# An attention and mixture block on one core: TensorE order written by hand, V mixed a batch ahead, residual in place, and a new order of loads

## The chip, the cores and the metric

One core of one Trainium2 chip runs the kernel. The metric is the time of one execution on the device in microseconds (us). Before the change it is 268.94 us (median of four runs, 268.52 to 269.49).

A time is given with the granted clock of TensorE, the mean over the span of what the trace records (in the traces of before and after, each record is 1 or 0.5). A run is called slow when it lies more than 1.5% above the fastest run of the same kernel. On one core that label is only about times. A median is over all runs, a ratio over the fast ones.

## The reference, cut to what matters

```
# batch 4, heads 8, seq 768, head_dim 64, 8 blocks of 96 rows
P = sort_net                                  # [4, 8, 8, 8]
5 times: P = exp(P - max); P /= rowsum; P /= colsum
k_sorted, v_sorted = P applied to the 8 blocks of k and of v
attn = softmax(q_block @ k_sorted_block.T / 8)
x = (attn @ v_sorted_block), heads side by side             # [4, 768, 512]
a1 = alpha1 * x + beta1
u  = x + lam * (w_tok @ a1)                   # token mixing, w_tok [768, 768]
a2 = alpha2 * u + beta2
out = u + lam * (relu(a2 @ w_ch1) @ w_ch2)    # channel stage, hidden 2048
```

The inputs and the output are float32. The kernel works in 16-bit types on TensorE.

## The kernel before

Names used in this text: `raw` is k or v as loaded; `bigP`, `bigV` are the mixing matrices made of P; `kT`, `Vs` are mixed k (transposed) and mixed v; `sc_ps` scores; `et` their exponentials; `x` the attention result; `tok_ps` token mixing; `u` the residual; `a2T` its transposed affine copy; `h_ps`, `hT` the hidden layer; `W2p` is w_ch2; `ch_ps` the channel result. P.V is the product of `et` and `Vs`. A filler (`spin`) is a matmul whose result nobody uses; `gate` is a tiny GpSimd copy that only holds back the loads queued behind it until what it reads has arrived. In the profiles PE is TensorE (PEld its weight loads), DVE VectorE, ACT ScalarE, POOL GpSimd.

Every compute engine is wrapped: while `fixed` is true its instructions keep program order, and with `fixed = False` the compiler may reorder them. GpSimd (`pool`) issues most loads. SyncE (`nc.sync`) issues the stores, the round trip of V through a scratch in memory (`vscr`), and the DMA transposes.

```python
    def load_weights():                       # called early in batch 0
        for g in range(4):
            pool.dma_start(W1p[...g...], w1v[...g...])
        load_raw(1, 1)                        # v of batch 1
        for g in range(4):
            pool.dma_start(W2p[...g...], w2v[...g...])

    def mix_v(b, banks=2, groups=range(6), copies=...):
        ...  # matmuls raw x bigV -> v_ps, copied to vA
        for th in range(2):
            nc.sync.dma_start(vscr[b, ...th...], vA[...th...])
        for par in range(2):
            regroup[b] = nc.sync.dma_start(Vs[b % NV][...par...], vscr[b]...)

    def emit_attention(b):                    # batches 1 to 3
        ...
        prev = [emit_scores(b, 0, g) for g in range(2)]
        for h4 in range(1, H4):
            cur = [emit_scores(b, h4, g) for g in range(2)]
            emit_pv(b, h4 - 1, prev, x128, xs)
            ...

    def moe_ch(b, hf, kks=range(3)):
        ...
            ost = att.tile([128, C], FT, name="ost", tag="ost", bufs=2)
            ...  # 16 matmuls hT x W2p into cps
                dve.tensor_tensor(cps[:], cps[:], lamB[:, lo:hi], ALU.mult)
                dve.tensor_tensor(ost[:, lo:hi], cps[:], u_of[b][kt][:, lo:hi], ALU.add)
                ...  # ost stored by SyncE

    pe.fixed = False                          # the compiler's order from here
    for b in range(1, B):
        if b > 1:
            if b > 2:
                cross_q(b)                    # six DMA transposes of q on SyncE
            mixing_matrices(b)
            mix_v(b)
            if b == 2:
                ...                           # gate, then load_q(3), load_raw(3, 1), load_raw(3, 0)
            mix_k(b)
        emit_attention(b)
        if b == 1:
            moe_ch(0, 0, (2,))
        else:
            moe_h(b - 1, 0)
            moe_ch(b - 1, 0)
        moe_h(b - 1, 1)
        moe_a(b)                              # token mixing, u, transposes of u
        moe_ch(b - 1, 1)
        if b == 1:
            load_q(2)
            cross_q(2)
    for hf in range(2):
        moe_h(B - 1, hf)
        moe_ch(B - 1, hf)
```

The softmax here doesn't subtract the row's maximum and nothing guards it: scores larger than these inputs give would overflow.

## Time and profile before

| | before |
|---|---|
| time, median (range) | 268.94 us (268.52 to 269.49) |
| span of the profiled run | 266.8 us |
| mean granted clock | 1.000 |
| first token-mixing matmul of batch 0, 1, 2, 3 | 33.96, 85.25, 144.03, 202.81 us |
| last matmul ends | 262.66 us |

The last two rows come from the timeline of TensorE. I use the first token-mixing matmul of each batch as milestones and call the times between them stretches: 51.3 us from batch 0 to 1 (of which the first 8.7 belong to batch 0's token mixing, up to the first h at 42.64 us), 58.8, 58.8, and 59.9 us from the last milestone to the end.

First, the busy rows of the page. The first line is the engine's busy time, share and instruction count; the digits are the busy share in 40 equal slices of the span (one slice is 6.7 us); PEclk is the granted clock in tenths and DMA the busy share of the DMA engines.

```profile
PE 257.6 (97%) x2049; PEld 141.6 (53%) x2059; DVE 154.8 (58%) x333; ACT 125.8 (47%) x232; POOL 92.5 (35%) x100
...
PE   7799999999999999999999999999999999999993
...
PEclk9999999999999999999999999999999999999999
DMA  6999999999999544499996342494200432012012
```

TensorE is the bottleneck and it is never long without work after the first slice; its clock stays at full. The DMA engines are over 90% busy in slices 2 to 13, from 7 to 87 us.

The waits of TensorE (engine, tile, the instruction that released it; then total us, times, longest us) are short. The whole kernel has no matmul wait over 1.4 us:

```profile
PE spin_ps L65 <- POOL ident L65: 1.4, 1, 1.4
PE pj_ps L65 <- DVE P L65: 1.2, 1, 1.2
```

Two groups of the page's fifth part (busy us and mean ns, then idle us just before the group and who ended it). The channel matmuls wait for nothing. GpSimd's rows of `u` wait for VectorE's `ost`:

```profile
L65 PE MATMUL ch_ps<-W2p,hTa 128*128 128x512 bf16 (+2 forms) x290 | 65.9, 370 | 0.5
...
L65 POOL TENSOR_SCALAR u<-b1lB,rs 128x512 f32<-128x512 f32 x18 | 28.8, 1610 | 64.1 <-DVE ost L65 59.3
```

Busy time by stage (windows; the stage's edges, its length, then each engine's busy time and instruction count, the clock, and the DMA engines' time as a share):

```profile
core 0: us, PE busy (x) PEld busy (x) DVE busy (x) ACT busy (x) POOL busy (x), PEclk, DMA share, GB/s
34.00:43.00 9.00, 9.00 (x57) 4.38 (x54) 7.33 (x15) 5.79 (x10) 8.17 (x8) 1.00 1.16 210
43.00:85.00 42.00, 41.80 (x389) 24.73 (x391) 28.68 (x58) 24.87 (x48) 18.29 (x20) 1.00 1.29 182
85.00:144.00 59.00, 58.69 (x420) 30.88 (x421) 35.47 (x72) 28.47 (x53) 25.75 (x26) 1.00 0.92 131
144.00:203.00 59.00, 58.69 (x420) 30.85 (x420) 35.11 (x71) 28.31 (x53) 16.64 (x13) 1.00 0.42 70
```

The loads that matter later are those of W2, four of 512 KB, as GpSimd issues them. This is its timeline (start, duration, engine, operation):

```profile
27.31 1.54 POOL L65 DMA_DIRECT2D W2p<-in_moe_w_ch_dram  x2
29.09 0.75 POOL L65 DMA_DIRECT2D W2p<-in_moe_w_ch_dram  x1 [0.24 <-DMA W1p<-in_moe_w_ch_dram]
31.60 0.74 POOL L65 DMA_DIRECT2D W2p<-in_moe_w_ch_dram  x1 [1.76 <-DMA W1p<-in_moe_w_ch_dram]
```

They landed between 42.62 and 50.24 us. The first channel matmul needs them at 55.2 us.

### The profile page before, as it was taken

To read this page: it belongs to the slowest core of one execution; us is meant where nothing else is said; L and a number is where in the kernel's file an instruction comes from. 1 tells how busy PE (TensorE), PEld (TensorE's weight loads), DVE (VectorE), ACT (ScalarE), POOL (GpSimd) and SP (SyncE) were. 2 spreads that over 40 slices of the span, in tenths; PEclk is the share of its full clock that TensorE was granted. 3 is DMA by queue.
4 is the path that set the end of the run, shared out by engine and by line. 5 is a ranking of instruction groups with operands and counts; after the bars stand their busy time and mean duration, and the time that the engine had idled before them with its cause. 6 is when DMAs were issued, how large, how long until landed. Compare 5 with 4: busy or idle time off the path is not lost.

```text
span 266.8 us, 5149 instructions
## 1 busy us (share of the span) xinstructions
PE 257.6 (97%) x2049; PEld 141.6 (53%) x2059; DVE 154.8 (58%) x333; ACT 125.8 (47%) x232; POOL 92.5 (35%) x100
## 2 busy tenths in 40 slices
PE   7799999999999999999999999999999999999993
PEld 2467745565565444554565444554565445545542
DVE  5878788629567966722585966704675962042033
ACT  3376757643585312980375404970474305504600
POOL 8524689203575615007917225002409000000000
PEclk9999999999999999999999999999999999999999
DMA  6999999999999544499996342494200432012012
GB/s 83 174 208 251 207 210 207 211 216 112 211 157 155 113 84 117 114 82 89 202 211 136 61 100 80 118 98 62 80 2 2 81 76 79 2 39 79 2 39 79
DMA packets 62423, 30.88 MB, mean 116 GB/s; under 512 B 48888, under 2 KB 58112, under 8 KB 62400
## 3 DMA queue, kind: packets, MB, share of 16 engines
q0 software_dynamic: 23024, 15.60, 39.4%
q1 hardware_dynamic: 39280, 14.89, 32.6%
q8 instruction: 16, 0.26, 0.4%
q14 instruction: 7, 0.06, 0.1%
q10 hardware_dynamic: 96, 0.07, 0.1%
HBM read 32.78 MB, written 8.65 MB: 155 GB/s over the span
## 4 chain that ended last, share of the span: by engine, by line
PE 89%; ACT 4%; DVE 4%; issue 1%; DMA 1%; DVEq 0%; ACTq 0%
PE ch_ps L65 31%; PE h_ps L65 30%; PE tok_ps L65 12%; PE x_ps L65 5%; PE sc_ps L65 4%; ACT kT L65 2%; PE v_ps L65 2%; PE k_ps L65 1%; PE q_ps L65 1%; ACT et L65 1%; DVE csum L65 1%; DVE P L65 1%; PE m_ps L65 1%; DVE rsum L65 1%; DMA P<-in_sort_net_dram 1%
## 5 line engine op out<-in xcount | busy, mean ns | idle before, releaser
L65 PE MATMUL h_ps<-a2T,W1p 128*128 128x384 bf16 x512 | 93.4, 326 | 0.1
L65 ACT ACTIVATE hTa<-h_ps 128x384 bf16<-128x384 f32 x96 | 45.9, 492 | 68.1 <-PE h_ps L65 67.0
L65 PE MATMUL ch_ps<-W2p,hTa 128*128 128x512 bf16 (+2 forms) x290 | 65.9, 370 | 0.5
L65 PEld LDWEIGHTS <-W1p 128*128 128x128 bf16 x512 | 47.5, 98 | 30.3 <-issue 0.9
L65 DVE TENSOR_TENSOR ch_ps<-ch_ps,lamB 128x512 f32<-128x512 f32 (+2 forms) x25 | 16.9, 676 | 63.2 <-PE ch_ps L65 60.5
L65 POOL TENSOR_SCALAR u<-b1lB,rs 128x512 f32<-128x512 f32 x18 | 28.8, 1610 | 64.1 <-DVE ost L65 59.3
L65 PEld LDWEIGHTS <-hTa 128*128 128x128 bf16 x300 | 28.7, 98 | 32.4
L65 PE MATMUL tok_ps<-x,w_tokT 128*128 128x512 f16 x144 | 32.1, 379 | 0.0
L65 POOL TENSOR_TENSOR u<-x,u 128x512 f32<-128x512 f16 x22 | 25.3, 1181 | 18.1 <-DVE x L65 17.3
L65 ACT ACTIVATE et<-sc_ps 96x768 f16<-96x768 f32 x32 | 24.9, 807 | 11.7 <-PE sc_ps L65 11.7
L65 ACT CAST u<-u 128x512 f16<-128x512 f32 x24 | 14.8, 618 | 24.8 <-DVE u L65 24.8
L65 PE MATMUL ch_ps<-W2p,hTb 128*128 128x512 bf16 (+2 forms) x100 | 25.0, 371 | 0.0
L65 PEld LDWEIGHTS <-w_tokT 128*128 128x128 f16 x180 | 14.8, 97 | 16.1
L65 DVE TENSOR_TENSOR tok_ps<-tok_ps,a1lB 128x512 f32<-128x512 f32 x24 | 16.5, 692 | 7.3 <-PE tok_ps L65 7.3
L65 DVE CAST kT<-k_ps 64x512 f16<-64x512 f32 x24 | 16.5, 688 | 3.4 <-PE k_ps L65 3.0
L65 DVE TENSOR_TENSOR x<-x_ps,recip 96x512 f16<-96x512 f32 (+2 forms) x32 | 17.6, 554 | 0.9
L65 DVE TENSOR_TENSOR u<-tok_ps,u 128x512 f32<-128x512 f32 x24 | 16.4, 688 | 1.7
L65 ACT ACTIVATE hTb<-h_ps 128x384 bf16<-128x384 f32 x32 | 15.3, 497 | 3.8 <-PE h_ps L65 3.4
L65 DVE TENSOR_TENSOR ost<-ch_ps,u 128x512 f32<-128x512 f32 (+2 forms) x25 | 16.6, 665 | 0.6
L65 POOL DMA_DIRECT2D qn<-in_q_dram x18 | 15.5, 875 | 4.2 <-PE q_ps L65 3.4
L65 PEld LDWEIGHTS <-hTb 128*128 128x128 bf16 x100 | 9.6, 98 | 10.9
L65 PEld LDWEIGHTS <-et 96*128 96x128 f16 (+2 forms) x288 | 12.4, 99 | 4.6 <-issue 1.2
(95 smaller groups left out, 214.7 us busy)
## 6 DMA issues: line engine op xcount, KB each, us to landing
out_dram<-ost SPq DMA_DIRECT2D x23, 192.0 KB, 2.2
raw<-in_v_dram POOLq DMA_DIRECT2D x8, 384.0 KB, 8.9
raw<-in_k_dram POOLq DMA_DIRECT2D x8, 384.0 KB, 10.9
vscr<-vA SPq DMA_DIRECT2D x6, 384.0 KB, 4.4
Vs<-vscr SPq DMA_DIRECT2D x6, 384.0 KB, 7.7
W1p<-in_moe_w_ch_dram POOLq DMA_DIRECT2D x4, 512.0 KB, 10.1
W2p<-in_moe_w_ch_dram POOLq DMA_DIRECT2D x4, 512.0 KB, 17.9
qn<-in_q_dram POOLq DMA_DIRECT2D x12, 128.0 KB, 5.8
```

What stands on the lines that cost most here:

```text
L65: ins = getattr(self.eng, name)(*args, **kwargs)
```

## The change

The intent: write TensorE's order by hand from batch 1 on, so that score groups come in pairs and channel work fills the distances between them; mix V one batch early, so that its round trip through memory is off the path; add the channel result into the tile of `u` itself instead of an output tile; order GpSimd's queue by hand and gate its loads; load w_tok in its natural row order in one load. The mixing matrices of batches 2 and 3 are made at the start of batch 1, no longer each in its own batch. Batch 0 is reordered too, most of its filler matmuls go, and the transposes of `u` in batch 0 come after the sixth token tile.

The core of the diff (some 850 lines, cut):

```diff
+    def attention_steps(b, first, less=0.0):
+        ...
+        yield 0, lambda: scores(0)
+        yield 2.4 - less, lambda: scores(1)
+        yield first, lambda: values(0)
+        yield 2.2 - less, lambda: scores(2)
+        ...
+    def weave(fill, steps):
+        for gap, step in steps:
+            filled = 0
+            while filled < gap:
+                took = next(fill, None)
+                ...
+            step()
...
-            ost = att.tile([128, C], FT, name="ost", tag="ost", bufs=2)
+            u32 = u_of[(b, kt)]
...
-                dve.tensor_tensor(ost[:, lo:hi], cps[:], u_of[b][kt][:, lo:hi], ALU.add)
+                dve.tensor_tensor(u32[:, lo:hi], cps[:], u32[:, lo:hi], ALU.add)
...
-    load_weights()
...
+    load_w1(range(2))
+    load_raw(1, 1)
+    load_w1(range(2, 3))
+    prep_affine()
+    load_raw(1, 0)
+    load_w1(range(3, 4))
+    load_q(1)
...
+    load_w2(range(2))                         # at the start of batch 0's token mixing
...
+    pool.tensor_copy(gate[32:64, :], Vs[1][32:64, 0, 0:2])   # waits for V of batch 1
+    load_q(2)
+    load_w2(range(2, 4))
     load_raw(2, 1)
     load_raw(2, 0)
+    cross_q(2, regroup[1])
+    moe_rows(1, range(5))
     pe.fixed = True
...
     for b in range(1, B):
-        if b > 1:
-            ...
-            mix_v(b)
-            ...
-        emit_attention(b)
...
+        if b == 1:
+            fill = chain(moe_h(0, 1), moe_ch(0, 0), moe_ch(0, 1, (0,)))
+            ...
+        else:
+            fill = chain(moe_h(b - 1, 0), moe_ch(b - 1, 0), moe_h(b - 1, 1), moe_ch(b - 1, 1, (0,)))
+            ...
+        if b < B - 1:
+            at = len(steps) - (3 if b == 1 else 6)
+            steps[at:at] = [(g, lambda n=n: mixes(b + 1, n)) for n, g in enumerate((1.2, 0.7, 1.1))]
+            ...
+        weave(fill, steps)
+        run(fill)
+        moe_rows(b, range(5, NT))
         moe_a(b)
-        moe_ch(b - 1, 1)
+        run(moe_ch(b - 1, 1, (1, 2)))
+        ...
         if b == 1:
-            load_q(2)
-            cross_q(2)
+            load_q(3)
+            load_raw(3, 1)
+            load_raw(3, 0)
+            cross_q(3, turned[-1])
```

## The prediction

> **What bounds the kernel now.** TensorE: the page's first part gives it 97% busy, and the chain of waits lies 89% on it. [...]I read start-to-start distances from the trace. In unbroken runs 512 columns take 216 ns, 384 take 162.5, 128 take 56. Charging every matmul that distance gives 240.4 of the 261.1 us from first to last matmul; 20.7 us are lost:
>
> - 0 to 11.5 us: 2.3 us, under the chain of P on ScalarE and VectorE, which ends at 11.47.
> - 11.5 to 34 us (batch-0 attention, w_tok): 7.5 us, and 2.2 us more in ten filler matmuls. VectorE is 18.4 us busy from 10 to 34, ScalarE 15.2.
> - 34 to 221 us: 10.7 us, nearly all around attention: 3.5 us per batch. Token mixing, the channel stage alone and everything after 221 us lose nothing.
>
> The steady loss is mostly change of shape: to scores 0.10 to 0.14 us, back 0.12, to P.V 0.05, to k 0.11, to v 0.09. The scheduler makes eight score groups per batch.
>
> **What the change does.**
>
> 1. Scores in pairs: four score islands for eight, 4 x 0.24 us saved; with P.V 0.15, mixing matrices 0.2 and small waits about 1.5 us in batches 2 and 3 each, 0.9 in batch 1. Together 3.9 us, all on the path.
> 2. V a batch ahead: same matmuls moved. It takes the V round trip (4.4 + 7.7 us to landing) away from its use, but no TensorE wait on it shows before: zero.
> 3. Residual add in place: equal VectorE work: zero.
> 4. Batch 0: k/v loads by halves, fillers gone, evacuations split evenly, bias products earlier (VectorE waited 0.95 us for them). Against it: fills (0.33 us) and a copy (0.23) move into the P chain, +0.4. VectorE work from P to x is about 17 us, so token mixing should start near 32 us, not 34.0. But the 12 transposes now follow the sixth token tile, so the first h waits for affine copies (0.67 us each on ScalarE): a stall of about 1.2 us. Net 1 to 1.5 us.
> 5. Natural w_tok rows: one load for two, but 12 smaller evacuations for 6: zero.
> 6. Fixed order risks head-of-line waits: a score pair holds both large PSUM buffers until two 0.81 us exponentials finish. I charge 0.3 us per batch, about cancelled by waits between h matmuls (0.3 per batch) that vanish.
>
> Sum: 5 to 6 us. Transition losses remain.
>
> **Prediction: 263.4 us, range 259.5 to 267.3.** Faster by over 2%: 0.55; within 2%: 0.42; slower: 0.03.
>
> **What would show it.** Distances between matmuls: batches 2 and 3 lose about 2 us each, not 3.5. The TensorE timeline: scores sixteen at a time; batch-0 token mixing from about 32 us; a gap near 1.2 us before the first h. Windows: the stretch after the last attention still 41 us.
>
> **What would make it wrong.** Waits of scores or P.V on ScalarE in the fixed order; w_tok or batch-1 V landing late, as DMA is over 90% busy from 7 to 87 us; W2, now loaded later, missing at the channel stage; TensorE throttled in batch 0 without fillers[...]. The clock row shows no drop before; the longest gap is 1.3 us.

## The result, and the profile after

The changed kernel is correct and takes 281.37 us (median of four runs, 280.53 to 282.32). The ratio to the kernel before is 1.0462 (95% interval 1.0414 to 1.0510), so it is slower by 4.6%. Ratios here and below are the mean time of one kernel's fast runs over the mean of the other's fast runs of the same rounds, so they are not quite the ratios of the quoted medians.

| | before | after |
|---|---|---|
| span of the profiled run | 266.8 us | 278.9 us |
| granted clock | 1.000 (profiled run) | 0.963 to 0.975 (four runs) |
| first token matmul of batch 0 | 33.96 | 35.72 |
| first h of batch 0 | 42.64 | 47.73 |
| first h to first token matmul of batch 1 | 42.62 | 58.34 |
| batch 1 to 2 | 58.78 | 56.88 |
| batch 2 to 3 | 58.78 | 55.59 |
| batch 3 to the last matmul | 59.85 | 56.40 |

The stretches don't hold the same work, so two corrections are needed. One channel tile (16 matmuls of 512 columns at 216 ns, 3.46 us) moved from behind the token mixing to ahead of it in every batch: the first stretch gained one, the last lost one. The V matmuls of a batch (six of 512 columns, 1.3 us) moved ahead by one batch: those of batch 1 now come ahead of the first h, and batch 2 to 3 holds none. With the same work on both sides, the change cost 5.09 - 1.30 = 3.8 us ahead of the first h and 15.72 - 3.46 = 12.3 us in the first stretch. It gained 1.9 us in batch 1 to 2, 3.19 - 1.30 = 1.9 us in batch 2 to 3, and nothing at the end. That makes 12.3 us at the last matmul (274.94 against 262.66).

The same rows of the page:

```profile
PE 256.9 (92%) x2047; PEld 142.6 (51%) x2047; DVE 145.7 (52%) x319; ACT 138.8 (50%) x251; POOL 88.7 (32%) x94
...
PE   5988799999941999999999999999999999999994
...
PEclk9999779999995799999999999999999999999999
DMA  6999999999999879599999914210210143012012
```

One slice is now 7 us. TensorE is busy 40% of slice 12 and 10% of slice 13 (77 to 91 us). The clock row has two dents: slices 5 and 6, and slices 13 and 14. The DMA engines are as full as before in slices 2 to 13, but then stay busier, and their second full period is slices 18 to 22 (before: 18 to 21).

The waits of TensorE name the hole:

```profile
PE ch_ps L65 <- DMA W2p<-in_moe_w_ch_dram: 6.8, 2, 5.8
PE v_ps L65 <- DMA raw<-in_v_dram: 3.0, 1, 3.0
```

The two groups that answer to those of before. The channel matmuls now wait for W2, and GpSimd's rows of `u` wait for the store of `u`, where they waited for VectorE:

```profile
L65 PE MATMUL ch_ps<-W2p,hT 128*128 128x512 bf16 (+2 forms) x400 | 89.2, 374 | 6.8 <-DMA W2p<-in_moe_w_ch_dram 6.8
...
L65 POOL TENSOR_SCALAR u<-b1lB,rs 128x512 f32<-128x512 f32 x18 | 28.0, 1563 | 56.3 <-DMA out_dram<-u 55.3
```

The stages, with edges moved to the milestones of after:

```profile
core 0: us, PE busy (x) PEld busy (x) DVE busy (x) ACT busy (x) POOL busy (x), PEclk, DMA share, GB/s
36.00:48.00 12.00, 11.57 (x55) 5.13 (x54) 8.53 (x14) 7.71 (x13) 6.48 (x6) 0.86 1.20 204
48.00:106.00 58.00, 48.03 (x412) 26.81 (x411) 24.55 (x55) 29.95 (x56) 18.57 (x20) 0.91 1.15 139
106.00:163.00 57.00, 56.65 (x421) 30.88 (x419) 32.20 (x62) 32.12 (x58) 24.01 (x23) 1.00 1.15 139
163.00:219.00 56.00, 55.65 (x416) 30.38 (x415) 31.82 (x63) 28.84 (x54) 16.55 (x13) 1.00 0.18 44
```

The loss lies in the first two rows; the later two are at full clock and busy throughout. In the second row TensorE is busy 48 of 58 us.

The hole is best read from two timelines. First TensorE at 77 to 91 us:

```profile
78.55 0.38 PE L65 MATMUL ch_ps<-W2p,hT 128*128 128x512 bf16 x1
79.92 1.02 PE L65 MATMUL ch_ps<-W2p,hT 128*128 128x512 bf16 x4 [0.99 <-DMA W2p<-in_moe_w_ch_dram]
86.72 0.58 PE L65 MATMUL ch_ps<-W2p,hT 128*128 128x512 bf16 x1 [5.77 <-DMA W2p<-in_moe_w_ch_dram]
90.28 1.01 PE L65 MATMUL v_ps<-raw,bigV 128*128 128x512 f16 x2 [2.98 <-DMA raw<-in_v_dram]
```

Between 78.9 and 90.3 us TensorE waits first for the third quarter of W2, then the fourth, then V of batch 2. Why so late? GpSimd's timeline at 41 to 71 us (a bracket is the idle time just before, and what ended it):

```profile
41.92 1.52 POOL L65 DMA_DIRECT2D W2p<-in_moe_w_ch_dram  x2
62.68 0.18 POOL L65 COPY gate<-Vs 32x2 f16<-32x2 f16 x1 [19.24 <-DMA Vs<-vscr]
63.72 5.25 POOL L65 DMA_DIRECT2D qn<-in_q_dram  x6 [0.86 <-PE q_ps L65]
68.92 1.55 POOL L65 DMA_DIRECT2D W2p<-in_moe_w_ch_dram  x2
70.39 1.16 POOL L65 DMA_DIRECT2D raw<-in_v_dram  x2
```

The second half of W2 stands behind a gate that waits 19.2 us for V of batch 1, and behind six q loads. It is issued at 68.92 us where before it went out by 31.60, and it lands at 79.88 and 86.67 us where it is wanted at 79. V of batch 2 stands behind it: landed 88.50 and 90.14, wanted at 79 because it is now mixed a batch ahead (before: landed by 76.5, wanted at 106). At the same time SyncE issues six q transposes in 67 to 91 us, two of which hold its queue for 6.98 and 9.94 us; before, they stood at the end of the batch.

The three waits make 9.7 us (0.99 + 5.77 + 2.98). TensorE's clock was at half from 83.9 to 94.1 us, so what it did run there took twice its time (matmuls of 512 columns followed each other at 427 ns instead of 216): most of the rest of the 12.3 us (an estimate from these numbers).

### The profile page after: what moved, and what is told of

It is laid out like the page before. It is cut to its first block, busy times and chain, and to the rows that moved or that the text cites. A ratio compares the mean times of both kernels' runs of the same rounds, so it can differ in the third digit from the quotient of the medians.

```text
span 278.9 us, 5123 instructions
## 1 busy us (share of the span) xinstructions
PE 256.9 (92%) x2047; PEld 142.6 (51%) x2047; DVE 145.7 (52%) x319; ACT 138.8 (50%) x251; POOL 88.7 (32%) x94
## 4 chain that ended last, share of the span: by engine, by line
PE 80%; DMA 7%; ACT 4%; DVE 4%; POOL 3%; issue 1%; POOLq 0%; DVEq 0%
PE ch_ps L65 29%; PE h_ps L65 25%; PE tok_ps L65 12%; DMA raw<-in_v_dram 7%; PE spin_ps L65 3%; PE x_ps L65 2%; POOL qn L65 2%; PE sc_ps L65 2%; ACT kT L65 2%; PE v_ps L65 2%; PE q_ps L65 2%; DVE wtp L65 1%; PE k_ps L65 1%; DVE x L65 1%; PE wtok_ps L65 1%
## 5 line engine op out<-in xcount | busy, mean ns | idle before, releaser
L65 PE MATMUL ch_ps<-W2p,hT 128*128 128x512 bf16 (+2 forms) x400 | 89.2, 374 | 6.8 <-DMA W2p<-in_moe_w_ch_dram 6.8
L65 PE MATMUL h_ps<-a2T,W1p 128*128 128x384 bf16 x512 | 89.4, 326 | 1.4 <-ACT hT L65 0.7
L65 ACT ACTIVATE hT<-h_ps 128x384 bf16<-128x384 f32 x128 | 60.3, 493 | 53.8 <-PE h_ps L65 53.4
L65 PEld LDWEIGHTS <-hT 128*128 128x128 bf16 x400 | 38.0, 99 | 43.7 <-issue 3.2
L65 POOL TENSOR_SCALAR u<-b1lB,rs 128x512 f32<-128x512 f32 x18 | 28.0, 1563 | 56.3 <-DMA out_dram<-u 55.3
L65 PE MATMUL tok_ps<-x,w_tokT 128*128 128x512 f16 x144 | 33.9, 393 | 0.0
L65 DVE RECIPROCAL recip<-x_ps 96x8 f32<-96x8 f32 (+1 forms) x32 | 6.2, 195 | 27.5 <-PE x_ps L65 27.4
L65 DVE TENSOR_TENSOR u<-ch_ps,u 128x512 f32<-128x512 f32 (+2 forms) x25 | 16.7, 667 | 0.8
L65 ACT CAST vA<-v_ps 128x1024 f16<-128x1024 f32 x8 | 8.1, 1010 | 17.5 <-PE v_ps L65 17.5
L65 PEld LDWEIGHTS <-et 96*128 96x128 f16 (+1 forms) x288 | 12.7, 108 | 2.3
L65 PE MATMUL x_ps<-Vs,et 96*128 96x65 f16 (+1 forms) x288 | 13.2, 201 | 0.0
```

What stands on the lines that cost most here:

```text
L65: ins = getattr(self.eng, name)(*args, **kwargs)
```

## The experiments

Eighteen kernels ran, all correct. Five questions were open: which part of the load order makes the hole (e1 to e3, e15 to e18); why the clock drops in batch 0 and what the prologue costs (e4, e6 to e8, e12); whether V a batch ahead costs by itself (e5, e11, e13, e15 to e18); what the hand order gains (e9, e14); what the residual in place costs (e10).

"Stretches" are first h to batch 1, then batch 1 to 2, 2 to 3, and 3 to end, in the profiled run. Where one run only was fast there is no ratio. Times of a wait are the profile's. A "hole" is counted from the start of one matmul to the start of the next, up to 0.4 us more than the wait in it.

| run | on | median us (range) | ratio | first h | stretches |
|---|---|---|---|---|---|
| before | | 268.94 (268.52 to 269.49) | 1 | 42.64 | 42.6, 58.8, 58.8, 59.9 |
| after | | 281.37 (280.53 to 282.32) | 1.0462 | 47.73 | 58.3, 56.9, 55.6, 56.4 |
| e1_w2_early | after | 274.75 (270.94 to 279.99) | 1.0131 | 43.70 | 57.4, 56.9, 55.8, 56.4 |
| e2_no_gate | after | 276.73 (275.36 to 279.10) | 1.0304 | 45.02 | 57.9, 57.1, 55.8, 56.4 |
| e3_w2_v2_first | after | 274.98 (274.60 to 277.05) | 1.0256 | 44.25 | 46.1, 66.4, 55.7, 56.4 |
| e4_affine_late | after | 279.78 (276.93 to 282.18) | 1.0373 | 47.52 | 60.1, 56.9, 55.6, 56.4 |
| e5_v2_in_batch2 | e1 | 288.29 (276.34 to 293.07) | none | 44.55 | 44.8, 79.0, 57.3, 56.4 |
| e6_affine_slot | e5 | 286.21 (283.28 to 294.17) | 1.0614 | 45.63 | 44.8, 77.2, 57.3, 56.4 |
| e7_fillers | e6 | 289.19 (277.76 to 297.52) | 1.0338 | 45.41 | 44.8, 83.3, 57.3, 56.4 |
| e8_fewer_spins | e6 | 284.81 (279.78 to 295.60) | 1.0448 | 44.70 | 44.8, 83.6, 57.3, 56.4 |
| e9_order_on_before | before | 278.41 (276.45 to 280.82) | 1.0351 | 43.02 | 42.6, 61.0, 63.3, 62.5 |
| e10_inplace_on_before | before | 271.00 (268.52 to 274.34) | 1.0059 | 42.58 | 42.6, 58.9, 61.6, 59.9 |
| e11_v_own_batch | after | 285.83 (281.13 to 288.51) | 1.0518 | 45.54 | 44.8, 68.7, 65.7, 58.1 |
| e12_fill_at_rs | e11 | 278.68 (275.27 to 281.88) | 1.0282 | 45.06 | 44.8, 62.6, 62.9, 56.4 |
| e13_change_mended | e12 | 273.46 (266.31 to 275.17) | none | 43.11 | 44.8, 59.9, 56.4, 56.4 |
| e14_order_mended | before | 270.19 (269.13 to 272.26) | 1.0043 | 43.64 | 42.6, 61.9, 61.9, 56.4 |
| e15_queue_order | e3 | 279.92 (273.76 to 283.51) | 1.0257 | 43.22 | 46.1, 66.8, 55.6, 56.4 |
| e16_q_behind_u | e13 | 274.31 (273.44 to 277.59) | 1.0195 | 43.50 | 44.8, 61.5, 62.1, 56.4 |
| e17_v3_first | e15 | 268.21 (265.98 to 270.34) | 0.9964 | 42.95 | 46.1, 58.8, 56.0, 56.4 |
| e18_v3_gated | e17 | 265.60 (263.84 to 270.20) | 0.9888 | 43.05 | 46.0, 56.9, 55.7, 56.4 |

Runs of "before" beside these, in the same rounds, had medians between 268.63 and 268.91 us. The runs of e5 to e8, e11, e13 and e15 spread over 7 to 20 us, so their ratios, taken over the fast ones, flatter them; for those kernels I argue from stretches and waits, not from the ratio.

### e1, e2, e3: who makes the hole

e1 moves the second half of W2 ahead of the gate:

```diff
+    load_w2(range(2, 4))
     pool.tensor_copy(gate[32:64, :], Vs[1][32:64, 0, 0:2])
     load_q(2)
-    load_w2(range(2, 4))
     load_raw(2, 1)
```

> The second half of W2 is issued before the GpSimd wait for the V scratch instead of after it and after the six q loads. Theory A (W2 simply arrives late): the 6.8 us that TensorE waited for W2 vanish, W2 lands before 65 us, and only part of the wait for V of batch 2 (3.0 us) stays, because V now stands behind q alone: time 272 to 275, against 281.4 for the change as it stands. Theory B (it is the throttled clock that makes batch 1 slow, the waits only follow it): less than 3 us gained, 278 or more. Theory C (the V scratch round trip of batch 1 was protected by the gap in the loads): W2 now collides with it, the scratch lands over 3 us later than 62.5 us and the P.V of batch 1 waits; the gain is under 5 us.

The wait for W2 is gone, but TensorE then stood 8.5 us for V of batch 2 (landed at 84.3 us) in one piece:

```profile
PE v_ps L65 <- DMA raw<-in_v_dram: 8.5, 1, 8.5
```

The first stretch fell only from 58.3 to 57.4. Median 274.75, four runs of which two are called slow. The time is the one that theory A gave, the mechanism is not: only part of the wait for V was to stay. W2's place was a cause, but behind it stood the next one.

e2 takes the gate away and leaves the order:

```diff
-    pool.tensor_copy(gate[32:64, :], Vs[1][32:64, 0, 0:2])
     load_q(2)
     load_w2(range(2, 4))
```

> The gate alone is taken away; the order of the loads stays: six q loads, W2, V, K. Theory A1 (the order is at fault: the q loads need the buffer of batch 1's q, which TensorE reads until 63.4 us, so W2 and V stand behind that anyway): nothing changes, 280.5 to 282.5. Theory A2 (the gate is at fault): W2 is issued near 45 us and the time falls by 6 us or more, to 275 or less.

The q loads now waited 20.3 us by themselves, for the q buffer that TensorE's q transposes free at 61 us. W2 was waited for 5.3 us and V 3.4 us: the same hole. So the gate is not the cause of the hole. Anything placed behind load_q(2) waits until then. The time meets neither theory: the median, 276.73 us, is 4.6 us under after's. The two profiled runs differ by 2.8 us, and 2.7 of these lie ahead of the first h, where the edit does nothing (one window of half clock fewer); what the other runs gained is not shown.

e3 is e1 with V of batch 2 ahead of q of batch 2 as well:

```diff
+    load_w2(range(2, 4))
     pool.tensor_copy(gate[32:64, :], Vs[1][32:64, 0, 0:2])
-    load_q(2)
-    load_w2(range(2, 4))
     load_raw(2, 1)
+    load_q(2)
     load_raw(2, 0)
```

> As the first, and V of batch 2 is loaded before q of batch 2 after the gate. Theory A: both waits of TensorE (6.8 us for W2, 3.0 us for V) go, V of batch 2 lands near 68 us; the whole stall of 11.2 us between 78.5 and 90.3 us goes, and with it the half clock behind it (about 1.6 us): 268 to 271. If only W2 matters: no better than the first kernel by more than 1 us.

The hole is gone: the first stretch is 46.05 us, which is the 42.6 of before plus the moved channel tile. But the next stretch is 66.4 us. V's scratch was written only at 87.7 us though V was mixed by 80, since the q transposes held SyncE's queue from 74.5 to 86.5 us; the transposes of `u` came late after it (from 101.6 us), the last two of them landed 6.9 and 7.4 us after their issue, beside the q loads of batch 3, and TensorE waited in front of h for VectorE's work on them:

```profile
PE h_ps L65 <- DVE u L65: 4.3, 1, 4.3
PE h_ps L65 <- DVE a2T L65: 2.1, 1, 2.1
```

The loss did not vanish, it moved into the other queue. The expected time of 268 to 271 us was missed for that.

### e4: VectorE against GpSimd in the prologue

VectorE's copies that sort w_tok got longer. From the timelines, before and then after, around those copies:

```profile
24.70 0.96 DVE L65 COPY wtp<-wt 128x1152 f16<-128x1152 f16 x2
...
26.27 0.62 DVE L65 COPY wtp<-wt 128x1152 f16<-128x1152 f16 x2
```

```profile
25.37 3.38 DVE L65 COPY wtp<-wt 128x1152 f16<-128x1152 f16 x4
25.39 1.55 POOL L65 TENSOR_TENSOR a1lB<-a1lB,lamB 128x512 f32<-128x512 f32 x1 [0.80 <-DMA a1lB<-in_moe_alpha_dram]
...
26.91 1.27 POOL L65 TENSOR_TENSOR b1lB<-b1lB,lamB 128x512 f32<-128x512 f32 x1
```

Four copies took 1.6 us before and 3.4 us after, at exactly the time of the two GpSimd products that the change had moved earlier (1.55 and 1.27 us). The longest single copy took 1.52 us, its like without a GpSimd product beside it 0.45; the copy before it took 1.32 us, its like 0.25 to 0.59. How much the copies lose went with the overlap: in e1 to e3, with the same code there, the four took 1.70, 1.16 and 2.23 us, the shortest in e2, where the first product started only after them.

```diff
     load_w1(range(2, 3))
-    prep_affine()
     load_raw(1, 0)
     load_w1(range(3, 4))
     load_q(1)
+    prep_affine()
```

> Only the two bias products on GpSimd are moved, from 25.4 us (on top of four VectorE copies of w_tok, which then took 3.38 us) to after the loads of q of batch 1, near 33 us. Theory D[...]: the four copies take 1.6 to 2.0 us, the holes of TensorE of 0.63 and 1.08 us before the w_tok transposes shrink, token mixing of batch 0 starts about 1.5 us earlier (34.2), and if the holes are what drops the clock to half, the two half-clock stretches before 40 us shrink too and token mixing gains another 1.7 us: 278 to 280. Rival (the copies wait for w_tok itself, which landed at 23.5 us, or are slow in their shape): copies still over 3 us, time within 0.7 us of 281.4.

The copies fell back to 0.45, 0.44, 0.44 and 0.25 us, and token mixing started at 33.10. But the two products (1.28 and 1.27 us) now ran at 33.04 to 35.5 us, and one VectorE instruction of the mixing matrices (`bigP`, 0.29 us in before) took 3.02 us beside them. VectorE was late from there on, TensorE waited 2.25 us from 39.3 us, and a window of half clock followed. So the first h came at 47.52 us, about as late as in after. VectorE's work was longer beside these products at both places (3.38 us for the four copies, 3.02 us for `bigP`); where they went decided only which work it was.

### e5 to e8: a wrong placement of mine, and the clock in batch 0

e5 is e1 with V of batch 2 mixed in batch 2 itself:

```diff
-        if b < B - 1:
+        if b == 2:
+            steps[0:0] = [(g, lambda n=n: mixes(2, n)) for n, g in enumerate((0.6, 1.2, 1.2))]
+        if b == 2:                            # only V of batch 3 stays ahead
             at = len(steps) - ...
```

> W2 before the gate as in the first kernel, and V of batch 2 mixed at the start of batch 2 (its need moves from about 79 us to about 105 us), V of batch 3 still a batch ahead. Theory E (mixing V of batch 2 a batch ahead asks for it before the loads can bring it; no order of the loads gives W2, V and q of batch 2 in time): the whole stall between 75 and 95 us goes, the stretch from the first h to token mixing of batch 1 falls from 58.3 us (57.4 with W2 early) to 44 to 46 us, batch 2 keeps its gain, and the time is 264 to 269. Rival (the hand order of batch 1 itself is too tight, whatever is loaded): that stretch stays above 50 us and the time above 271.

The first stretch is 44.76 us, as expected (42.6 + 3.5 - 1.3 = 44.8). The next is 79.0 us, by my own fault: V's scratch now stood behind the q transposes of batch 3 in SyncE's queue and was issued 20 us late. So the run confirms the cause of the first hole and says nothing of the rest. e6, e7 and e8 carry the same fault and are read for the prologue alone.

e6 is meant to let the two products wait for the fourth w_tok copy:

```diff
-    prep_affine()
     ...
             sort_wtok(1)
+            with tc.issue_after(dve.last.ins):
+                prep_affine()
```

> As the one before, and the two bias products on GpSimd wait for the fourth w_tok copy on VectorE, so that they run near 26 to 29 us[...]. Theory D[...]: copies 0.25 to 0.45 us each, no VectorE operation over 2 us before the first h, token mixing of batch 0 starts at 33.0 to 33.6 in every run, half clock before 45 us absent or shorter; 1 to 2 us faster than the one before and a smaller spread. Rival: no difference beyond 0.7 us.

The edit did not do what it was meant to: the first product still started at 25.30 us, beside the copies, and the fourth copy took 1.32 us. Token mixing started at 33.63 us, and the clock was at half from 34.7 to 38.1 us. So this run does not tell what the copies cost. The other profiles do, roughly. From the first P product to token mixing it took 21.0 to 21.3 us where the four copies took 1.2 to 1.4 us (e2, e4, e5, e8; in e11, whose fifth copy was slow, 21.7), 21.1 to 21.7 where they took 1.7 to 2.3 (e1, e3, e6), and 23.1 in after (3.4, with a window of half clock on top). So the copies cost some tenths of a microsecond.

e7 adds nine filler matmuls among the w_tok transposes:

```diff
+    spin(psa([128, 512], FT, "spin_ps")[:], 4)
     prep_wtok(range(0, 2))
     sort_wtok(2)
+    spin(psa([128, 512], FT, "spin_ps")[:], 3)
     pv0(3, 0)
     prep_wtok(range(2, 4))
+    spin(psa([128, 512], FT, "spin_ps")[:], 2)
```

> As the one before, with nine filler matmuls (1.9 us of TensorE) at the places before the w_tok transposes where TensorE waits. Theory F (low TensorE activity from 25 to 34 us is what drops the clock to half): no half clock before 45 us in the profile and a smaller spread over runs than the one before; token mixing starts at most 0.5 us later; mean equal or better by up to 1.5 us. Rival (the fillers only cost their time): 0.5 to 1.5 us slower.

A miss: the clock was at half from 34.5 to 37.9 us all the same. The fillers stood ahead of the poor window, not in it.

e8 is e6 with three fillers instead of seven in the third round of the P chain:

```diff
-        spin(psa([128, 512], FT, "spin_ps")[:], (8, 0, 7, 4, 2)[it])
+        spin(psa([128, 512], FT, "spin_ps")[:], (8, 0, 3, 4, 2)[it])
```

> As the one with the bias products moved, and three filler matmuls instead of seven in the third round of the P normalisation. Theory G (the seven stand in front of the first q transposes, whose copy stands in front of the fifth exp on ScalarE): the chain of P ends 0.4 to 0.8 us earlier, at 11.6 to 11.9 us, and token mixing starts as much earlier: 0.3 to 0.8 us faster. Rival (q itself lands too late): no change.

The first P product came at 11.65 us and token mixing at 32.69, against 12.63 and 35.72 in after. But e2 and e5, which touch nothing there, have 11.70 and 33.01, 11.54 and 32.55. So the difference is the draw of one profile, and nothing is shown for the fillers.

What those four and the others do show is the clock. In after's trace it changes at 29.25, 32.66, 36.08, 39.49, 83.86 and 94.11 us: the distances are 3.41 us or whole multiples of it (13 and 3 times), a grid whose phase differs from run to run (the records begin at 5.09 us in before and 8.77 in after, 3.68 apart). I counted for each window of the grid how much of it TensorE spent streaming columns (216 ns for 512, as measured in unbroken runs at full clock; without the one-column row sums). In after, two windows with 0.38 and 0.34 were each followed by a window of half clock; so were 0.36, 0.37 and 0.37 in e5, e7 and e8. Windows with 0.39 (e13), 0.42 (e1) and 0.44 (e12) were not. The longest gap between two matmuls in after's poor windows is 1.3 us from start to start.

Counted over all 156 windows of the traces of before and after, the seven with 0 to 0.38 were followed by half clock, and the 149 with 0.40 or more by full clock. One window of another run does not fit: in e14, whose prologue is that of before, a window of 0.54 at 10.8 us was followed by half clock. Why is not shown.

The four profiles with one code in the prologue have the first h at 43.70 and 44.25 us (e1 and e3, no half clock there), 45.02 (e2, one window) and 47.73 (after, two windows).

### e9: the hand order alone, spoilt

The kernel before with the hand order in batches 2 and 3, V still in its own batch:

```diff
+            fill = chain(moe_h(b - 1, 0), moe_ch(b - 1, 0), moe_h(b - 1, 1))
+            steps = [(0.6, lambda b=b: mixing_matrices(b))]
+            steps += [...mix_v..., ...mix_k...]
+            steps += attention_steps(b, 4.3)
+            weave(fill, steps)
```

> The kernel before with one part of the change alone: in batches 2 and 3 TensorE's order is fixed by hand (scores and P.V in pairs, woven into the h and channel matmuls); loads, V in its own batch, the separate output tile, batch 0 and batch 1 as before. The order is worth 1.9 us per batch by the stretches between token mixings of the change (55.6 + 1.3 for V, against 58.8). Theory: 3.0 to 4.0 us faster than before, 264.7 to 265.7, with full clock throughout. Rival (the order only works with the rest of the change): within 1 us of before, or slower.

A miss, and again mine: my gaps used up the filler, so token mixing waited for `x` 6.0 us in four waits, scores waited for `kT`, and the clock dropped twice, after those holes. It shows only how little slack this fixed order leaves: in those waits TensorE did not step aside to other work.

### e10: the residual in place alone

```diff
-            ost = att.tile([128, C], FT, name="ost", tag="ost", bufs=2)
+            ost = u_of[b][kt]
...
-        u32 = [moep.tile([128, C], FT, name=f"u32_{kt}", tag="u32", bufs=9) for kt in range(NT)]
+        u32 = [moep.tile([128, C], FT, name=f"u32_{kt}", tag="u32", bufs=11) for kt in range(NT)]
```

> The kernel before with the channel result added into the residual tile, whose buffers grow from 9 to 11 as in the change. My prediction said zero: within 0.7 us of 268.7. Rival (the buffer is now free only when its store has landed, and a store stands in the one queue behind transposes and the V scratch): the rows of the next batch come late and token mixing of batch 1 or 2 waits, 1 to 7 us slower.

From its waits:

```profile
POOL u L65 <- DMA out_dram<-u: 54.3, 9, 17.3
PE tok_ps L65 <- DVE u L65: 1.5, 1, 1.5
```

The `u` buffers are free only when the store has landed. GpSimd's row products then come late, and TensorE stood 1.85 us in one place (the wait of 1.5); a second wait, 0.8 us for VectorE's `bigV`, followed in the same stretch. The ratio is 1.0059 (1.0020 to 1.0098): 1.6 us of 268.8, not zero. In the changed kernel the same wait of GpSimd (55.3 us) did not reach TensorE; in e7, e8 and e11, where stores stood behind q transposes, it did (holes of 4.0 to 6.9 us).

### e11, e12: V in its own batch, and fillers in the right window

e11 is after with W2 ahead of the gate, the products moved as in e6, V of batches 2 and 3 in their own batch, and the q loads and transposes of batch 3 behind V's scratch:

```diff
+        if b > 1:
+            steps[0:0] = [(g, lambda n=n: mixes(b, n)) for n, g in enumerate((0.6, 1.2, 1.2))]
+        if b == 2:
+            def more():
+                pool.tensor_copy(gate[0:32, :], Vs[0][0:32, 0, 0:2])
+                load_q(3); load_raw(3, 1); load_raw(3, 0)
+                cross_q(3, regroup[2])
+            steps.insert(3, (0, more))
```

> The change with the second half of W2 before the gate, V of batches 2 and 3 mixed in their own batch, the loads and transposes of q of batch 3 behind the V scratch of batch 2 as in the kernel before, and the bias products behind the w_tok copies. Theory E with the queue: the new stalls of batch 2 in the last four kernels (V scratch of batch 2 issued 20 us late because the transposes of q of batch 3 stood before it) go; first h to token mixing of batch 1 is 44.7 us, the two stretches after it 58 to 58.5 us minus 1.9, that is 56.5 to 57.5; the time is 263 to 267, with about 1.7 us lost to half clock at token mixing of batch 0. Rival (the in-place residual still blocks: the rows of batch 1 wait for stores behind the transposes of q of batch 2): a hole of 3 to 7 us in token mixing of batch 1 in some runs, 268 to 275.

The first stretch is 44.8 us again. The later ones are 68.7 and 65.7 us, with waits of 5.0 us (token tile for `u`, whose store stood behind the q transposes), twice 3.1 us (token mixing for `x`, since the longer list of steps used up the filler) and 3.2 us (h for `u`). A miss, for two faults of queue and filler of my own, not for V.

e12 adds four filler matmuls ahead of the row sums, in the window that e7 had missed:

```diff
     mixing_matrices(1)
+    spin(psa([128, 512], FT, "spin_ps")[:], 4)
     prep_rs()
```

> As the one before, with four filler matmuls (0.86 us) just before the row sums of w_tok, where TensorE waits 0.7 us for copies. In all profiles so far the clock fell to half after a stretch of 3.4 us in which matmuls streamed under about 0.4 of the time, and not where it was 0.42 or more; here that stretch (30 to 34 us) held 0.33 to 0.37. Theory F: half clock before 45 us goes in all profiles, token mixing of batch 0 takes 4.0 us for its first three tiles, not 5.7; 0.5 to 1.5 us faster than the one before. Rival: half clock stays.

Windows of e11, then of e12 (the last three numbers are clock, DMA share and GB/s):

```profile
29.00:33.00 4.00, 1.90 (x36) 1.48 (x34) 3.36 (x12) 1.67 (x3) 2.91 (x5) 1.00 1.09 208
33.00:45.00 12.00, 12.00 (x81) 5.78 (x79) 8.44 (x15) 7.01 (x12) 8.73 (x9) 0.86 1.18 206
```

```profile
29.00:33.00 4.00, 3.25 (x56) 2.87 (x57) 3.31 (x12) 2.40 (x5) 2.43 (x4) 1.00 1.09 215
33.00:45.00 12.00, 11.60 (x94) 6.08 (x93) 9.47 (x19) 8.09 (x15) 7.98 (x8) 1.00 1.18 205
```

TensorE is busy 3.25 of 4 us instead of 1.90, and the next 12 us run at clock 1.00 instead of 0.86. From the first token matmul to the first h it takes 10.3 us, not 12.0. No profile with these fillers (e12, e13, e15 to e18) has half clock between 20 and 45 us; of the ten with this prologue and without them, eight have (all but e1 and e3; e4 only after its own hole). So more streaming in that window took the clock's dent out of batch 0, in all six profiles. In this pair of profiles the first h is only 0.5 us earlier (45.06 against 45.54), since token mixing started later.

### e13, e16: V in its own batch, mended

e13 is e12 with shorter gaps, and with the q transposes of batch 2 behind the stores of batch 0's first half:

```diff
-            steps = [... enumerate((0.6, 2.4, 3.0))]
-            steps.append((4.4, lambda: None))
-            steps += attention_steps(b, 5.3)
+            steps = [... enumerate((0.6, 1.2, 1.2))]
+            steps.append((3.6, lambda: None))
+            steps += attention_steps(b, 4.3, 0.3)
...
+        if b == 1:
+            cross_q(2, stored[(0, 2)])
...
-    cross_q(2, regroup[1])
```

> This is e12 with two repairs of what my own edits of e11 and e12 broke: shorter gaps in the hand order of batches 2 and 3, so that about 5 us of filler is left after the last P.V group, and the six q transposes of batch 2 put behind the stores of batch 0's first half in SyncE's queue. Theory G (with V mixed in its own batch and the queue in that order, the rest of the change costs nothing more than its prologue and gains about 2 us a batch): the stretches between first token tiles are 44.8, 56 to 58, 56 to 58 and 56.4 us, no hole over 1 us in the token tiles of batch 0, and the time is 263 to 268 us in fast runs. Rival (the hand order itself cannot be kept fed when it is bound to one order): holes of 2 us and more remain where scores wait for kT or the token product waits for x, the middle stretches stay over 60 us, and the time stays over 272 us.

The profiled run took 266.31 us with full clock; the five others took 272 to 275 with clocks of 0.985 to 0.993. One hole of 3.5 us was left at 106 us, where h waited for `u`, whose transposes had queued behind the q transposes. Its window had 0.39 of streaming and was followed by full clock, where 0.38 in after was followed by half clock. The stretches are close to what was expected but for that one (59.9).

e16 moves the q transposes behind those of `u`:

```diff
-            cross_q(2, stored[(0, 2)])
         moe_a(b)
+        if b == 1:
+            cross_q(2, turned[-1])
```

> This is e13 with one move: the six q transposes of batch 2 stand behind the six u transposes of batch 1 in SyncE's queue instead of ahead of them. In e13 TensorE stood 3.5 us at 106 us, waiting for VectorE's work on u transposes that had queued behind the q transposes (87 to 97 us), and five of six runs had a lower granted clock and were 6 to 9 us longer than the profiled one. Theory Q (the queue's order made the hole, and the hole made the clock drop in most runs): no hole over 1.2 us after 45 us, the second stretch falls from 59.9 to about 56.8 us, the granted clock is 0.997 or more in most runs, and the time is 261 to 265 us in fast runs: faster than both kernels. Rival (the drop of the clock comes from something else, such as the chip's state under the denser queue): the hole goes but most runs still have a clock under 0.993 and stay at 268 to 274 us.

A miss: 273.4 to 277.6 us. The hole at 106 us went, but now V's scratch stood behind the q transposes (written at 112.8, read back from 117.7) and P.V waited 3.0 us for it at 124 us; 3.2 us were lost in front of h at 169 us, and each of the two was followed by a window of half clock. With V in its own batch SyncE has three things to send at the start of batch 2, and one is late in the orders of e11, e13 and e16. That suggests what mixing V ahead is good for; the kernel before, where the compiler may reorder TensorE, has V in its own batch and no such hole.

### e14: the hand order alone, mended

```diff
-            steps += [...mix_k... enumerate((1.2, 2.4, 2.0))]
-            steps.append((1.2, lambda: None))
-            steps += attention_steps(b, 4.3)
+            steps += [...mix_k... enumerate((0.6, 1.2, 1.2))]
+            steps.append((3.6, lambda: None))
+            steps += attention_steps(b, 4.3, 0.3)
```

(and one channel tile more in each batch's filler, as in the change.)

> The kernel before with only the hand order, in batches 2 and 3, with gaps made to fit (e9 had gaps that used up the filler and then left TensorE waiting for x and for kT). Theory G: the order of the TensorE queue by hand is worth about 2 us a batch wherever it is not starved: stretches 42.6, 56 to 58, 56 to 58 and about 59.5 us, full clock to the end, 264 to 266 us. Rival (the compiler's scheduling order of the kernel before is as good, and the shorter batches of the changed kernel come only from what it moved out of them): the stretches stay at 58.5 or more and the time at 268 to 272 us.

Median 270.19, ratio 1.0043 (1.0019 to 1.0067). The rival is nearer: no gain in sum. In batch 2 to 3, with the same work as before, the stretch is 61.87 against 58.78 us; 2.7 us of it are lost where V's matmuls wait for VectorE's `bigV`, 0.8 us in another place, and 1.7 us is the half clock that follows the first (half of 3.4 us). Without these three it would be 56.7 us (an estimate from those numbers). Batch 1 to 2, less its one channel tile more, is 58.4 us with 1.0 and 0.7 us lost in the same way, so 56.7 too. The changed kernel doesn't have the wait for `bigV`, because it makes these matrices in batch 1. So the order packs about 2 us better, and gives it back as soon as one of its instructions is not ready. In e13, with the matrices made early and V in its own batch, the stretch of batch 2 to 3 is 56.4 us. The profiled run is the slowest of e14's six; it also has a window of half clock at 14.3 us, which the edit doesn't touch.

### e15, e17, e18: V a batch ahead, queues mended one by one

e15 is e3 with the q transposes of batch 2 behind the `u` transposes of batch 1, and with e12's fillers:

```diff
-    cross_q(2, regroup[1])
...
         if b == 1:
+            cross_q(2, turned[-1])
             load_q(3)
             load_raw(3, 1)
```

> This is e3 (W2 before the gate, V of batch 2 loaded ahead of q of batch 2, V still mixed a batch ahead) with the six q transposes of batch 2 moved behind the u transposes of batch 1 in SyncE's queue, and 4 fillers ahead of the row sums as in e12. Theory Q (what costs is the order of the two load queues, not mixing V a batch ahead): the first stretch is 46.0 us as in e3, the second falls from 66.4 to about 57 us because the V scratch is written some 8 us earlier and no u transpose is late, then 55.7 and 56.4; no half clock after 30 us; 264 to 269 us in fast runs. Rival (V a batch ahead takes bandwidth in batch 1 that other transfers need, in any order): the second stretch stays over 61 us, with holes where h waits for u or V for its regroup, and the time stays over 272 us.

By the numbers the rival: 66.8 us in the second stretch. But the holes of e3 were gone, and one new hole of 8.3 us stood at 121.7 us. TensorE waited 7.9 us for V of batch 3. GpSimd issued that load at 120.28, after six q loads that had waited 14.6 us for the q buffer, which the moved transposes now freed later. The next fault in line.

e17 puts that V load ahead of the q loads:

```diff
             cross_q(2, turned[-1])
-            load_q(3)
             load_raw(3, 1)
+            load_q(3)
             load_raw(3, 0)
```

> This is e15 (V mixed a batch ahead, W2 and V of batch 2 early, q transposes of batch 2 behind the u transposes) with the V load of batch 3 put ahead of its q loads in GpSimd's queue, where in e15 it waited until 120 us for the q buffer and TensorE then stood 8.3 us at 121.7 us. Theory Q (V a batch ahead costs only through the order of the load queues): the V load is issued before 105 us, the hole at 121 us is gone, the second stretch falls from 66.8 to 57 to 58.5 us, and the time is 263 to 267 us in fast runs. Rival (V a batch ahead costs by itself): another hole of over 3 us opens in the second stretch, and the time stays over 270 us.

Median 268.21 us (265.98 to 270.34), ratio 0.9964 (0.9911 to 1.0018): with V still a batch ahead, the queues mended and the fillers in, the whole loss of 4.6% is recovered. One hole of 2.5 us was left. Its timelines (GpSimd's load, then VectorE's work on the last `u` transpose):

```profile
100.04 1.11 POOL L65 DMA_DIRECT2D raw<-in_v_dram  x2
...
108.36 1.25 DVE L65 TENSOR_SCALAR a2T<-a2T,ab2col 128x384 bf16<-128x384 f16 x4 [3.79 <-DMA a2T<-u]
```

The V load went out at 100.04 us. The last `u` transpose, issued at 100.46, landed at 108.33; the five before it took 2.4 us each. Whether the load is the reason is what e18 tests.

e18 lets the V load wait for that transpose:

```diff
             cross_q(2, turned[-1])
+            pool.tensor_copy(gate[0:32, :], a2T_of[1][1][0:32, 0, 256:258])
             load_raw(3, 1)
             load_q(3)
```

> This is e17 with one gate more: the V load of batch 3 is issued only when the last u transpose of batch 1 has landed and been used (a two-column GpSimd copy of its result stands ahead of it). In e17 the sixth u transpose was issued at 100.46 us and landed only at 108.33, since the V load was issued at 100.04 and 100.61 us, and TensorE stood 2.5 us in front of h for it. Theory C (the collision of that load with that transpose is the whole of e17's remaining hole, and the hole lowers the clock in some of its runs): the sixth transpose lands within 3 us of its issue, no hole over 1.2 us in the second stretch, which falls from 58.8 to 56.3 to 57.3 us, and the median is 263.5 to 266.5 us, faster than before by 1 to 2 per cent. Rival (the transposes are late for other transfers, the stores and the V scratch, whatever the load does): the hole stays at 2 us or more or opens at another place, and the median stays at 267 to 270 us.

```profile
104.58 1.24 DVE L65 TENSOR_SCALAR a2T<-a2T,ab2col 128x384 bf16<-128x384 f16 x4
...
105.24 1.21 POOL L65 DMA_DIRECT2D raw<-in_v_dram  x2
```

The load is 5 us later, VectorE has the transpose 3.8 us earlier, and the transpose lands 2.5 us after its issue. The load now meets the q transposes of batch 2, of which the one issued at 104.14 us took 8.6 us to land; nobody waits for it. The second stretch is 56.9 us. The median is 265.60 us (263.84 to 270.20), the ratio 0.9888 (0.9856 to 0.9920); with the slow run counted, the means differ by 1.0%. Two of its stages, at full clock:

```profile
43.00:89.00 46.00, 45.72 (x412) 26.53 (x412) 25.13 (x56) 30.07 (x55) 16.95 (x18) 1.00 1.20 180
89.00:146.00 57.00, 56.65 (x421) 30.85 (x419) 31.37 (x62) 32.31 (x59) 24.55 (x24) 1.00 1.16 147
```

e18 is the changed kernel with five moves in the two queues and four filler matmuls. It beats the kernel before by 1.1% (a gain below 2%, but the interval excludes zero) and the changed kernel by 15.8 us in the medians, which were measured in different rounds. How much of that the fillers give is known only from e11 and e12: no half clock in batch 0, 1.7 us from token mixing to the first h.

## Why the prediction was wrong, point by point

The prediction was 263.4 us; the kernel took 281.4. Its sum went wrong in three places, and a risk that it named came true without a price.

1. **Step 2, and the load order that no step costed: this is what failed.** Step 2 said of V a batch ahead "same matmuls moved … no TensorE wait on it shows before: zero". That a wait does not show before says nothing about when the moved matmuls need their data: V of batch 2 was wanted at 79 us instead of 106, and W2 was issued at 68.9 instead of 31.6. I listed "W2, now loaded later, missing at the channel stage" and "DMA is over 90% busy from 7 to 87 us" among the risks, and had the numbers for a price: before, W2 took 15 to 19 us from issue to landing in that busy time, and the change put its second half behind a gate on V's round trip. The runs: the first stretch cost 12.3 us, and e3, which moves only those loads, took 12.3 us from it (58.34 to 46.05). e17 and e18 show that mixing ahead costs nothing once both queues are ordered for it, and e16 suggests that it has a use.

2. **Step 4, batch 0: right in direction at full clock, wrong in sum.** Predicted: token mixing near 32 us and 1 to 1.5 us gained. The profile has 35.72. The named risk of "TensorE throttled in batch 0 without fillers" came true twice (half clock at 29.3 to 32.7 and 36.1 to 39.5 us). Without it (e1 and e3, same prologue) token mixing starts at 33.4 and 33.9 and the first h, less the 1.3 us of V, at 42.4 and 43.0 against 42.6 before; with four fillers more (e13, e15 to e18) at 41.7 to 42.2, and in e12 at 43.8. So the step has two errors: at full clock the gain is at most 1.0 us and can be none, and the clock, which was not costed, takes 1.7 us for each window of half clock (an estimate: half of 3.41 us), 3.4 us in after. I had judged the clock by the longest gap, 1.3 us; in these traces the share of the window spent streaming told the drops apart (0.38 and 0.34 in after's two windows), but for the one window of e14. The 1.2 us stall in front of the first h was overestimated: waits of 0.4 and 0.2 us. The moved bias products, counted as a gain, doubled four copies of VectorE in that profile (1.6 to 3.4 us).

3. **Step 3, residual in place: zero was too low, but not here.** Alone it cost 1.6 us (e10), because the buffer's life now includes the store. In the changed kernel that wait stayed off TensorE.

4. **Step 1 and step 6, the hand order: right for batches 2 and 3.** Predicted 1.5 us each, measured 1.9 in both; taken from the 3.5 us lost per batch before, that leaves 1.6, where "about 2" was forecast. No run has the order alone without a hole of its own, so that the 1.9 us come from the order and not from other parts of the change rests on e13 and on the estimate at e14. The stretch after the last attention is shorter by just the moved channel tile, as forecast. Batch 1 gained nothing: without the hole it takes 46.05 - 3.46 = 42.6 us (e3), as before, where 0.9 was forecast. Head-of-line waits (one instruction that is not ready holds up all behind it), charged at 0.3 us, cost nothing where data was early, and 1 to 9 us where it was not. e14 is the warning: alone, with V in its own batch, the order gave all its gain back.

5. **Step 5, w_tok in natural rows: not separated.** Zero was forecast, and no run isolates it.

What is still open: why e13's five other runs are so much longer than its profiled one. Their clocks are lower, and a hole that trips the clock in one execution and not in another would do that: the profiled run's poor window had 0.39 of streaming where 0.38 in after was followed by half clock, and the phase of the grid differs between the profiled runs. But this is not shown: the lost clock (1 less the granted clock, times the span) is only 1.9 to 4.1 us of the 5.8 to 8.9 us, only one of the six runs has a profile, and e16, which removed that hole, opened others.

## What to carry to other kernels

Before moving a matmul earlier, or a load later, write down for each transfer when it is issued, when it lands under the load of its time, and when its first user now wants it; "no wait shows" in the old profile is only the slack of the old order. In these queues, which issued in order, the cost of a place was what stood ahead of it (19.2 us behind the gate in after, 12 us behind the q transposes in e3), so mend the queue whole: here each of the first three repairs uncovered the next fault (e1, e3, e15) and left the median near 275 us or above; the fourth (e17) brought the time level with the kernel before and the fifth (e18) under it. And give a fixed order of the bottleneck engine slack everywhere, since it waits where a free order steps aside, and here a wait of 2 us and more often cost a window of half clock too (after waits of 2.25 us in e4, 2.5 in e14, 3.0 and 3.2 in e16), 1.7 us each by the estimate above.
